# Moving the first step of a float64-to-float32 conversion from VectorE to ScalarE in a fused attention and gated-MLP kernel, with a new order of all instructions

## The chip, the core and the metric

The kernel runs on one core of a Trainium2 chip. Five engines work side by side, each in the order of its own instruction queue: TensorE (PE in the profile; its weight loads are PEld), VectorE (DVE), ScalarE (ACT), GpSimd (POOL) and SyncE (SP), which issues nearly all DMA transfers. The metric is the device time of one execution in microseconds, and the median over several executions is compared.

## The reference

A recurrence with decay runs over 768 positions for 4 x 8 heads of width 48, and its output goes through a gated MLP with 384 inputs and 1536 hidden units, for all 3072 tokens:

```python
for t in range(S):
    state = alpha[:, :, t, :, None] * state + np.einsum('bhd,bhe->bhde', k[:, :, t], v[:, :, t])
    y[:, :, t] = np.einsum('bhd,bhde->bhe', q[:, :, t], state)
...
g = x @ w_gate
silu = g * (1.0 / (1.0 + np.exp(-g)))
val = x @ w_val
return (silu * val @ w_out).astype(np.float32)
```

q, k, v and alpha are float32. The three weight matrices reach the kernel as float64, that is as pairs of 32-bit words, because they were drawn as float32 and then scaled with a float64 number.

## The kernel before, in words

**Attention.** The sequence is cut into 16 units of 192 positions (4 per batch element), each of three chunks of 64. The words of a unit u in the order table are: loads `La`, `Lk`, `Lq`, `V`; for the first four units a widening copy `pa`, `pk`, `pq` (L382), a transposition on TensorE `Ta`, `Tk`, `Tq` (L394) and evacuations `ea`, `ek`, `cq` (L798); for the later units a transposition on VectorE (`tr`, `tk`, `tq`, L374). `G` is the backward scan of the decays (L439) and `f` the forward scan after it (L445, L448), with a small reset `z`. `mk` and `q` multiply k and q with the scanned decays. `S` are the scores, `ma` their masking (L567), `K` and `kc` turn k and copy it out of PSUM, `B` and `Bw` form the carries between chunks, `ad` and `de` advance the state, `Y` are the outputs. `yh` and `yl` split an output into a high part rounded to float32r and the rest, and `R`, `x` (on chip) or `xr` (by DMA) lay it out as the MLP's input tile xT. Two units make one block of 384 tokens.

**MLP.** 96 steps s go over 8 blocks and 12 slices f of 128 hidden units. Blocks 0 and 1 alternate: steps 0 to 6 are block 0 with f 0 to 6, steps 7 to 13 block 1 with the same f, then f 7 to 11 of both. `g` and `v` are the products with the gate and the value weights, nine matmuls each, since both operands are split into high and low parts and three of the four combinations are used; `sl` is the silu on ScalarE (L710), `h` the product on VectorE (L714), `hh` and `hl` its high and low part (L718, L723), `o` the nine matmuls with `w_out` (L734). Each of `g` and `v` has one PSUM bank, so `v` of a step waits for `h` of the step before.

**Weights.** 36 pieces of 128 x 384 weights are loaded once, in 20 groups; groups 0, 1, 2 and 19 hold one piece (384 words per partition), the others two (768). Group 0 is the gate slice of f 0, 1 the value slice of f 0, 2 the gate slice of f 1, 3 the value slice of f 1 and the output slice of f 0, and so on. `wl` loads the raw words; the raw words of a group lie in the place of the next group's result, so that one cannot be written before the other is converted. Three conversion steps `w..v0`, `w..v1`, `w..v2` build a float32 word in a tile t (three buffers, shared with the range checks), all on VectorE (L148, L151, L154). `w..a` rounds it to float32r (L321), `w..p` subtracts for the low part (L325). Later each piece is loaded a second time (`wr`) and its range checked by ScalarE (`wc`, two activations that add up what lies outside, L296 and L297). If the sums are not as they should be, a slower general path runs behind the main one. `Lc` and `ck` do the same for alpha.

**What sets the order.** The table `ORDER` lists every word with its engine (t TensorE, v VectorE, s ScalarE, g GpSimd, y SyncE) and, behind @, the PSUM banks. The words are issued in the table's order, each engine runs its own in that order, and semaphores hold an instruction until its operands are there. Nothing is reordered.

Of the kernel before, what the change touches and what calls it, by code (L numbers as in the profile page):

```python
# [44 lines left out]
v:G0 s:w1a y:Lk1 s:pa1 y:La2 s:pq0 t:Ta1@01 v:w1p y:Lk2 t:Tq0@23 v:f0 g:z0 s:pk0 y:V0 t:Tk0@45 s:pq1 v:q0 g:pk1 g:w0p
v:mk0 t:Tk1@23 s:ea1 y:Lq2 s:ek1 t:Tq1@45 v:G1 y:La3 t:S0@01 y:wl2 s:qc0 y:wl3 t:K0.0@2 s:pa2 t:K0.2@3 v:f1 g:z1
s:kc0.0 t:K0.1@6 y:Lk3 s:vc0 y:wl4 s:kc0.1 y:wl5 v:ma0.2 g:mk1 s:kc0.2 t:Ta2@26 s:pa3 y:wl6 t:Bw0@1 v:w2v0 s:cq1
v:w2v1 y:wl7 v:w2v2 g:q1 t:K1.2@3 v:ma0.0 s:ad0.1 t:K1.1@4 t:K1.0@5 v:ma0.1 s:kc1.2 y:wl8 s:kc1.1 v:w3v0 s:qc1 t:S1@34
v:w3v1 s:ad0.2 v:w3v2 y:wl9 s:ea2 v:de1 s:ad0.0 t:Ta3@02 v:G2 s:kc1.0 t:Y0@16 y:wl10 s:pk2 s:w3a v:f2 g:z2 t:Bw1@5
s:yh0.0 y:V2 s:yh0.1 s:vc1 v:yl0.0 g:w3p s:ad1.0 v:ma1.0 s:ad1.1 v:ma1.2 v:yl0.1 t:Tk2@14 g:pq2 v:ma1.1 t:R0.2@6 g:w2a  # L50
v:mk2 s:ad1.2 s:x0.2 v:w2p t:Y1@35 v:w4v0 v:w5v0 t:Tq2@14 v:w5v1 y:V3 s:yh1.0 t:R0.1@6 s:yh1.1 v:w6v0 s:cq2 v:w4v1
s:pk3 t:K2.1@1 v:w4v2 t:R0.0@4 s:x0.1 s:kc2.1 t:K2.0@6 v:yl1.1 g:q2 s:w4a t:K2.2@1 v:x0.0 v:yl1.0 t:Tk3@45 s:kc2.0
y:Lq3 v:de2 s:kc2.2 y:wl11 t:R1.1@3 s:ea3 t:R1.2@6 v:w6v1 y:wl12 t:R1.0@1 v:w6v2 s:x1.2 t:S2@02 s:vc2 y:wl13 v:G3
# [88 lines left out]
def single(nc, raw, t):  # L142

    lo, hi = raw[:, :, 0], raw[:, :, 1]
    return [
        lambda: nc.vector.tensor_scalar(  # L148
# [958 lines left out]
```

## Time and profile before

| What | Value |
|---|---|
| Median of 3 executions | 576.37 us (576.31 to 577.98) |
| The profiled execution's own time | 574.98 us |
| Its span, first to last instruction | 573.2 us |
| Busy: PE, DVE, ACT, POOL | 546.3, 385.0, 248.4, 147.0 us |
| Mean granted TensorE clock | 0.989 |
| HBM read, written | 62.52 MB, 5.90 MB |

A row of a group of instructions reads: line, engine, operation, output and input tiles, shape, count, then total busy time and the mean of one in ns, then the idle time before them and what released most of it. A row of the timeline reads: start, duration, engine, line, operation, count, and in brackets the idle time before it with its releaser. A row of the table by stages gives the stretch and its length, the busy time and count of PE, PEld, DVE, ACT and POOL, the granted clock, the DMA share and GB/s. The chain gives start, length and what it was.

### The profile page before, as it was taken

To read this page: it belongs to the slowest core of one execution; us is meant where nothing else is said; L and a number is where in the kernel's file an instruction comes from. 1 tells how busy PE (TensorE), PEld (TensorE's weight loads), DVE (VectorE), ACT (ScalarE), POOL (GpSimd) and SP (SyncE) were. 2 spreads that over 40 slices of the span, in tenths; PEclk is the share of its full clock that TensorE was granted. 3 is DMA by queue.
4 is the path that set the end of the run, shared out by engine and by line. 5 is a ranking of instruction groups with operands and counts; after the bars stand their busy time and mean duration, and the time that the engine had idled before them with its cause. 6 is when DMAs were issued, how large, how long until landed. Compare 5 with 4: busy or idle time off the path is not lost.

```text
span 573.2 us, 13708 instructions
## 1 busy us (share of the span) xinstructions
PE 546.3 (95%) x5510; PEld 527.2 (92%) x5510; DVE 385.0 (67%) x596; ACT 248.4 (43%) x573; POOL 147.0 (26%) x169
## 2 busy tenths in 40 slices
...
GB/s 238 270 307 250 247 125 145 43 115 81 86 147 164 136 117 107 124 91 145 170 169 191 172 181 132 179 110 102 207 125 123 128 151 63 94 76 59 0 1 47
...
## 3 DMA queue, kind: packets, MB, share of 16 engines
...
HBM read 62.52 MB, written 5.90 MB: 119 GB/s over the span
## 4 chain that ended last, share of the span: by engine, by line
PE 88%; DVE 4%; ACT 2%; SPq 2%; issue 1%; DMA 1%; DVEq 0%; ACTq 0%
PE v L702 26%; PE ops L734 26%; PE g L702 25%; PE A L557 3%; PE y L629 2%; PE s L533 2%; PE pt L394 1%; SPq L686 1%; PE y L612 1%; PE y L613 1%; DVE t L154 1%; DVE t L151 1%; DMA raw<-in_moe_w_val_dram 1%; DVE w L325 1%; PE s L557 1%
## 5 line engine op out<-in xcount | busy, mean ns | idle before, releaser
L702 PE MATMUL v<-xT,w 128*128 128x384 f32 x864 | 167.6, 338 | 3.3 <-DVE h L714 3.3
L702 PE MATMUL g<-xT,w 128*128 128x384 f32 x864 | 166.9, 337 | 0.0
L734 PE MATMUL ops<-w,hh 128*128 128x384 f32 x576 | 158.8, 337 | 0.0
L702 PEld LDWEIGHTS v<-xT,w 128*128 128x128 f32 x864 | 150.5, 188 | 5.2 <-DVE h L714 4.4
L702 PEld LDWEIGHTS g<-xT,w 128*128 128x128 f32 x864 | 150.9, 188 | 0.6
L723 POOL TENSOR_TENSOR hl<-h,hh 128x384 fp32r<-128x384 f32 x67 | 70.5, 1052 | 250.3 <-ACT hh L718 236.0
L714 DVE TENSOR_TENSOR h<-h,v 128x384 f32<-128x384 f32 x96 | 53.0, 552 | 119.0 <-PE v L702 106.6
L718 ACT CAST hh<-h 128x384 fp32r<-128x384 f32 x96 | 49.0, 512 | 150.9 <-DVE h L714 77.5
L734 PEld LDWEIGHTS ops<-w,hh 128*128 128x128 f32 x576 | 105.3, 188 | 0.9 <-ACT K L497 0.2
L734 PE MATMUL ops<-w,hl 128*128 128x384 f32 x288 | 96.7, 336 | 0.0
L710 ACT ACTIVATE h<-g 128x384 f32<-128x384 f32 x96 | 47.0, 490 | 114.1 <-PE g L702 102.9
L508 DVE STREAM_TRANSPOSE K<-Gs 32x384 f32<-32x384 f32 x96 | 54.7, 570 | 5.4 <-PE A L557 3.8
L734 PEld LDWEIGHTS ops<-w,hl 128*128 128x128 f32 x288 | 54.1, 188 | 0.0
L567 DVE TENSOR_TENSOR X<-s,mask 64x384 f32<-64x384 f32 (+1 forms) x48 | 26.0, 550 | 5.8 <-DMA wc<-in_moe_w_out_dram 3.4
L439 DVE TENSOR_TENSOR_SCAN Gs<-AT,inj 128x772 f32<-128x772 f32 x16 | 29.0, 1814 | 1.1 <-ACT AT L798 0.8
L448 DVE TENSOR_TENSOR_SCAN AT<-AT,back 128x771 f32<-128x771 f32 x16 | 29.2, 1824 | 0.7
L723 DVE TENSOR_TENSOR hl<-h,hh 128x384 fp32r<-128x384 f32 x29 | 16.1, 557 | 16.3 <-ACT hh L718 16.2
L394 PE MATMUL pt<-ident,wide 128*128 128x128 f32 x72 | 14.2, 352 | 13.1 <-ACT wide L382 8.2
L394 PEld LDWEIGHTS pt<-ident,wide 128*128 128x128 f32 x72 | 10.7, 181 | 15.4 <-POOL sel L348 5.1
L452 POOL MEMSET AT<- 128x3 f32 x16 | 1.7, 106 | 89.1 <-DVE AT L448 89.1
L297 ACT ACTIVATE wc<-wc,wbias 128x384 f32<-128x384 f32 x36 | 23.3, 647 | 1.2
L325 POOL TENSOR_TENSOR w<-t,w 128x768 fp32r<-128x768 f32 (+1 forms) x11 | 19.1, 1744 | 15.3 <-ACT w L321 15.0
...
## 6 DMA issues: line engine op xcount, KB each, us to landing
...
raw<-in_moe_w_gate_dram SPq DMA_DIRECT2D x12, 384.0 KB, 8.0
raw<-in_moe_w_val_dram SPq DMA_DIRECT2D x12, 384.0 KB, 7.8
...
raw<-in_moe_w_out_dram SPq DMA_DIRECT2D x12, 384.0 KB, 7.8
wc<-in_moe_w_gate_dram SPq DMA_DIRECT2D x12, 384.0 KB, 5.0
wc<-in_moe_w_val_dram SPq DMA_DIRECT2D x12, 384.0 KB, 3.7
wc<-in_moe_w_out_dram SPq DMA_DIRECT2D x12, 384.0 KB, 3.9
```

Of the source, the lines that this page charges most:

```text
L325: eng.tensor_tensor(out=lo, in0=src, in1=hi.bitcast(F32), op=ALU.subtract)
L394: nc.tensor.transpose(pt[:, j - js.start, :], Wd.rearrange("p j e c -> p (j e c)")[:, j * P : (j + 1) * P], ident)
L439: nc.vector.tensor_tensor_scan(*(x.rearrange("p g t -> p (g t)")[:, ::-1] for x in (Gs, AT, inj)), 0.0, op0=ALU.mult, op1=ALU.add)
L448: nc.vector.tensor_tensor_scan(Af, Af, back[:, 1 : n + 1], back[:, 0:1], op0=ALU.mult, op1=ALU.add)
L508: nc.vector.transpose(out=bass.AP(k0.tensor, k0.offset, [k0.ap[0], (G * 2 * D, NU), (2 * D, G), (1, 32)]), in_=Kg[j * BO + x : j * BO + x ...
L567: nc.vector.tensor_tensor(out=X[r, z, f * GF : (f + 1) * GF, :].rearrange("r g (c t) -> r g c t", c=NU), in0=sps[f][r].rearrange("r g (c t ...
L702: nc.tensor.matmul(pt, wsp[kind, f][a][:, kt * P : (kt + 1) * P], xT[blk][:, b_, kt, :], start=(n == 0), stop=(n == 3 * KT - 1),)
L710: nc.scalar.activation(h, acc.pop(("g", blk, f)), AF.Silu)
L714: nc.vector.tensor_tensor(out=h, in0=h, in1=acc.pop(("v", blk, f)), op=ALU.mult)
L718: nc.scalar.copy(out=hh, in_=acc["h", blk, f])
L723: eng.tensor_tensor(out=hl, in0=acc.pop(("h", blk, f)), in1=hh.bitcast(F32), op=ALU.subtract)
L734: nc.tensor.matmul(ops[blk][i], h[b_][:, i * P : (i + 1) * P], wsp["o", f][a], start=(first and n == 0), stop=(last and n == 2),)
```

## The change

Three things are changed.

First, the conversion may begin on ScalarE. Before, VectorE's first step shifts the upper word left by 3 and sets bits, the second masks with the upper word, and the third brings in the top three bits of the lower word by a shift. Now, where the table names s for `w..v0`, ScalarE reads the lower word as a number, multiplies it with 7.49 / 2^32 and writes the result as an integer, 0 to 7, which stands for those three bits; VectorE then shifts the upper word, joins it, and masks. Where the table names v, VectorE does three steps as before, the last two exchanged.

Second, since the bits that were set before are now taken from the word itself, the range check must also exclude large weights. It takes |x|, then the distance from the middle of the permitted range, then what this exceeds half the range by: three activations instead of two.

Third, the order was searched anew, with an eighth PSUM bank (`ops2`) open for the early transpositions, turned pieces of k and outputs; the dummy matmuls, of which the table held none, are removed with the bank that they kept.

```diff
+W_LEAST, W_MOST = 4.0e-5, 1.9999
+W_MID, W_DEV = (W_MOST + W_LEAST) / 2, (W_MOST - W_LEAST) / 2
+LOW3 = 7.49 / 2.0 ** 32
...
 ORDER = """
-y:La0 y:wl0 y:wl1 y:Lq1 y:La1 y:Lq0 y:Lk0 s:pa0 y:V1 t:Ta0@01 v:w0v0 v:w0v1 s:ea0 v:w0v2 v:w1v0 v:w1v1 s:w0a v:w1v2
...
+y:La0 y:wl0 y:Lk1 y:La1 y:Lq0 y:V1 s:pa0 t:Ta0@01 s:w0v0 v:w0v1 s:ea0 v:w0v2 y:Lk0 s:w0a v:G0 s:pa1 y:Lq1 s:pq0 y:La2
...
     lo, hi = raw[:, :, 0], raw[:, :, 1]
...
+    def first(eng):
+        by.append(eng)
+        if eng is nc.scalar:
+            eng.activation(t, lo, AF.Copy, scale=LOW3)
+        else:
+            eng.tensor_scalar(
+                out=t, in0=hi, scalar1=3, scalar2=0xC0000001, op0=ALU.logical_shift_left, op1=ALU.bitwise_or
+            )
+
+    def second(eng):
+        if by[0] is nc.scalar:
+            eng.scalar_tensor_tensor(
+                out=t, in0=hi, scalar=3, in1=t, op0=ALU.logical_shift_left, op1=ALU.bitwise_or
+            )
+        else:
+            eng.scalar_tensor_tensor(
+                out=t, in0=lo, scalar=29, in1=t, op0=ALU.logical_shift_right, op1=ALU.bitwise_or
+            )
+
+    def third(eng):
+
+        eng.scalar_tensor_tensor(
             out=t, in0=hi, scalar=0x3FFFFFFF, in1=t, op0=ALU.bitwise_or, op1=ALU.bitwise_and
...
         nc.scalar.activation(dev, dev, AF.Abs, accum_out=wviol[:, 1, i : i + 1])
-        nc.scalar.activation(dev, dev, AF.Relu, bias=wbias, scale=-1.0, accum_out=wviol[:, 0, i : i + 1])
+        nc.scalar.activation(dev, dev, AF.Abs, bias=wbias[:, 0:1])
+        nc.scalar.activation(dev, dev, AF.Relu, bias=wbias[:, 1:2], accum_out=wviol[:, 0, i : i + 1])
...
-    BANKS = ("A0", "A1", "A2", "ops0", "ops1", "vps", "gps")
+    BANKS = ("A0", "A1", "A2", "ops0", "ops1", "vps", "gps", "ops2")
```

What the table now orders stands below at three places. A row names the line, the operation, the output and input tiles with their numbers, and the output's shape.

The first is the start of VectorE's queue, from the first conversion to the second backward scan (tiles: t and w are the conversion's and its result, Gs the scan's, AT the decays, pt a transposed bank, X a masked q, back the forward scan's factors). Before, the rows from the first conversion on:

```order
L148 TENSOR_SCALAR t0_155<-raw0_132 128x384
L151 SCALAR_TENSOR_TENSOR t0_155<-raw0_132,t0_155 128x384
L154 SCALAR_TENSOR_TENSOR t0_155<-raw0_132,t0_155 128x384
L148 TENSOR_SCALAR t1_161<-raw1_134 128x384
L151 SCALAR_TENSOR_TENSOR t1_161<-raw1_134,t1_161 128x384
L154 SCALAR_TENSOR_TENSOR t1_161<-raw1_134,t1_161 128x384
L439 SCALAR_TENSOR_TENSOR Gs0_167<-AT_86,inj_74 128x772
L325 TENSOR_TENSOR w1_169<-t1_161,w1_169 128x384
L445 RECIPROCAL back_89<-Gs0_167 128x4
L448 SCALAR_TENSOR_TENSOR AT_86<-AT_86,back_89 128x771
```

and now:

```order
L165 SCALAR_TENSOR_TENSOR t0_152<-raw0_132,t0_152 128x384
L175 SCALAR_TENSOR_TENSOR t0_152<-raw0_132,t0_152 128x384
L462 SCALAR_TENSOR_TENSOR Gs0_161<-AT_86,inj_74 128x772
L468 RECIPROCAL back_89<-Gs0_161 128x4
L471 SCALAR_TENSOR_TENSOR AT_86<-AT_86,back_89 128x771
L475 MEMSET AT_86 128x3
```

Group 0 has two steps there instead of three, and group 1 is converted after the second forward scan.

The second is ScalarE's queue around the evacuation of unit 2's decays (`ea2`, the rows that write AT). Before (kps and K: turned k and its copy; A2, s and SE: the carries and the state; wide: a widening copy):

```order
L473 COPY X1_104<-X1_104 48x384
L588 COPY SE_109<-s0_0_243 48x96 x2
L588 COPY SE_109<-A2_0_323 48x96 x2
L798 COPY AT_86<-pt2_0_0_311 128x4x32x3
L798 COPY AT_86<-pt2_0_1_315 128x4x32x3
```

and now:

```order
L496 COPY X1_104<-X1_104 48x384
L157 ACTIVATE t2_387<-raw2_221 128x384
L157 ACTIVATE t3_390<-raw3_223 128x768
L519 COPY K0_105<-kps1_0_315 64x4x48
L520 COPY K0_105<-kps1_0_315 64x4x48
L604 COPY V0_77<-A2_0_331 48x8x48
L604 COPY V0_77<-A2_0_331 48x8x48
L343 CAST w1_430<-t1_383 128x384
L343 CAST w2_435<-t2_387 128x384
L810 COPY AT_86<-pt2_0_0_285 128x4x32x3
L810 COPY AT_86<-pt2_0_1_289 128x4x32x3
```

Two first steps and two casts of the conversion, one turned piece and the advance of the state now stand between `qc1` and `ea2`; the copies into SE came before `ea2` and come after it now.

The third is TensorE's queue around the first gate product g0. Before (y: outputs of unit 2; kps3: a turned piece of unit 3's k):

```order
L629 MATMUL y1_2_855<-X0_103,U_101 48x64
L629 MATMUL y1_2_855<-X0_103,V0_77 48x64
L702 MATMUL g0_0_903<-xT0_587,w0_164 128x384 x9
L492 MATMUL kps3_1_920<-ident_91,Gs3_765 64x112 x4
L702 MATMUL v0_0_925<-xT0_587,w1_169 128x384 x9
L702 MATMUL g0_1_945<-xT0_587,w2_591 128x384 x9
```

and now:

```order
L515 MATMUL kps3_1_840<-ident_91,Gs3_750 64x112 x4
L725 MATMUL g0_0_845<-xT0_576,w0_159 128x384 x9
L725 MATMUL v0_0_867<-xT0_576,w1_430 128x384 x9
L635 MATMUL y0_2_890<-X0_103,V0_77 64x64
L636 MATMUL y0_2_890<-X0_103,V0_77 48x64
L635 MATMUL y1_2_891<-X0_103,V0_77 64x64
```

The outputs of unit 2 stood ahead of g0 and stand behind v0 now; one turned piece of unit 3's k has come ahead of it.

More of the change, by code (lines that the diff above doesn't have):

```diff
@@ L43 @@
 ORDER = """
-y:La0 y:wl0 y:wl1 y:Lq1 y:La1 y:Lq0 y:Lk0 s:pa0 y:V1 t:Ta0@01 v:w0v0 v:w0v1 s:ea0 v:w0v2 v:w1v0 v:w1v1 s:w0a v:w1v2
[L45 to L53, printed above, removed]
@@ new lines @@
+t:Ta1@01 y:V0 v:f0 t:Tq0@23 s:pk1 s:pk0 t:Tk1@45 v:z0 v:q0 t:Tk0@67 v:w0p s:qc0 y:wl1 v:mk0 g:pq1 s:ea1 y:wl2 y:wl3
+s:ek1 t:Tq1@23 v:G1 t:K0.0@0 y:wl4 s:pa2 t:S0@14 s:kc0.0 y:Lk3 v:mk1 t:K0.1@5 s:vc0 t:Ta2@67 y:La3 v:ma0.2 t:K0.2@0
+s:cq1 y:wl5 v:f1 t:K1.2@4 s:kc0.1 t:K1.0@2 y:wl6 t:K1.1@3 s:kc0.2 v:q1 t:Bw0@0 y:wl7 v:w1v0 s:qc1 v:w1v1 s:w2v0 v:w1v2
+s:w3v0 v:w2v1 y:wl8 s:kc1.0 v:w2v2 s:ad0.1 v:ma0.0 g:z1 t:S1@25 v:w3v1 s:w1a y:wl9 s:ad0.0 s:w2a v:ma1.2 g:pa3 s:ea2
+v:ma0.1 v:w1p s:ad0.2 t:Ta3@56 v:G2 y:Lk2 s:w4v0 t:Y0@01 y:Lq2 s:kc1.2 v:de1 s:kc1.1 y:wl10 v:f2 s:yh0.0 t:Bw1@3
@@ new lines @@
+s:yh0.1 y:V2 v:yl0.0 g:vc1 v:yl0.1 s:ad1.0 s:ad1.1 g:z2 v:ma1.0 t:R0.2@0 v:ma1.1 t:R0.1@1 v:w2p s:x0.2 t:Y1@47 s:ad1.2
+v:w4v1 v:w4v2 s:w5v0 s:x0.1 v:w5v1 t:R0.0@0 v:w5v2 s:yh1.0 s:pk2 y:wl11 v:yl1.0 s:pq2 v:w3v2 t:Tk2@12 s:w5a t:Tq2@34
+v:mk2 g:w4a s:w3a y:Lq3 y:wl12 s:x0.0 v:q2 g:w3p t:K2.2@1 s:yh1.1 t:K2.1@0 y:V3 s:kc2.2 t:K2.0@2 v:yl1.1 t:S2@34
+s:kc2.1 v:de2 s:ea3 t:R1.1@0 v:ma2.2 g:pk3 t:R1.0@1 s:kc2.0 v:x1.1 t:R1.2@4 v:G3 s:x1.0 t:Tk3@02 s:x1.2 t:Bw2@1 s:pq3
+y:wl13 s:vc2 v:mk3 y:wl14 s:w6v0 v:f3 t:Tq3@02 s:qc2 y:wl15 s:ad2.1 t:K3.1@4 t:g0 y:wl16 s:cq3 v:w6v1 y:wl17 s:kc3.1
```

206 lines of the change are left out of this document (94 added, 112 removed).

## The prediction

> **What bounds the kernel now.** I read the page's totals first, then the same totals by stage, then what TensorE (PE) waits for, then VectorE (DVE) in order of time.
>
> ```profile
> PE 546.3 (95%) x5510; PEld 527.2 (92%) x5510; DVE 385.0 (67%) x596; ACT 248.4 (43%) x573; POOL 147.0 (26%) x169
> core 0: us, PE busy (x) PEld busy (x) DVE busy (x) ACT busy (x) POOL busy (x), PEclk, DMA share, GB/s
> 0.00:26.00 26.00, 15.41 (x258) 13.16 (x258) 18.21 (x30) 17.63 (x36) 12.84 (x32) 1.00 0.83 242
> 26.00:34.00 8.00, 6.29 (x126) 5.46 (x128) 7.72 (x11) 5.67 (x14) 0.31 (x2) 0.60 1.08 368
> ...
> 44.00:48.00 4.00, 2.86 (x11) 2.86 (x12) 3.90 (x8) 2.98 (x7) 0.52 (x1) 0.58 0.43 67
> 48.00:56.20 8.20, 6.38 (x224) 5.49 (x223) 7.30 (x12) 6.19 (x15) 2.02 (x2) 1.00 1.01 348
> 56.20:97.30 41.10, 37.83 (x364) 35.56 (x361) 36.49 (x47) 19.32 (x40) 10.88 (x11) 1.00 0.70 177
> 97.30:300.00 202.70, 202.70 (x2203) 196.81 (x2204) 182.61 (x278) 58.19 (x127) 74.05 (x75) 1.00 0.49 121
> 300.00:550.00 250.00, 250.00 (x2088) 245.74 (x2087) 116.49 (x198) 128.26 (x312) 40.38 (x42) 1.00 0.44 121
> 550.00:573.20 23.20, 16.44 (x95) 16.12 (x93) 3.19 (x6) 4.46 (x9) 1.02 (x1) 0.94 0.08 29
> ```
>
> From 97.3 to 550 us PE is busy in every microsecond at the full granted clock. No TensorE work is added or removed, so that stretch cannot shrink; it can only start earlier, or gain holes. The idle of PE lies ahead of it (10.6 us before 26, about 9.6 us from 26 to 97.3) and in the last 23 us (6.8). The change therefore is worth what it does to the moment at which the dense stretch begins, which I mark by the product v7 (the first value product of block 1).
>
> ```profile
> 91.87 3.25 DMA L<-in_alpha_dram
> ...
> 95.25 0.06 DVE AT L374
> ...
> 96.67 0.56 DVE h L714
> ...
> 97.27 1.86 PE v L702 x9
> ```
>
> These are pieces of the chain of work that ended last. v7 starts at 97.27 because DVE's multiplication h6 ran at 96.67, behind a transposition (`tr4`) that waited for a load of alpha that SyncE had issued at 91.87. So in this stage DVE, and through it the DMA queue, releases PE. DVE's own order of time tells where it stood:
>
> ```profile
> 8.43 1.78 DVE L439 TENSOR_TENSOR_SCAN Gs<-AT,inj 128x772 f32<-128x772 f32 x1
> 15.54 1.77 DVE L439 TENSOR_TENSOR_SCAN Gs<-AT,inj 128x772 f32<-128x772 f32 x1 [0.85 <-ACT AT L798]
> 23.67 0.59 DVE L148 TENSOR_SCALAR t<-raw 128x384 uint32<-128x384 uint32 x1 [3.84 <-DMA raw<-in_moe_w_gate_dram]
> 29.72 1.77 DVE L439 TENSOR_TENSOR_SCAN Gs<-AT,inj 128x772 f32<-128x772 f32 x1
> 41.70 2.46 DVE L154 SCALAR_TENSOR_TENSOR t<-raw,t 128x768 uint32<-128x768 uint32 x1
> 48.11 1.76 DVE L439 TENSOR_TENSOR_SCAN Gs<-AT,inj 128x772 f32<-128x772 f32 x1
> 60.13 0.56 DVE L714 TENSOR_TENSOR h<-h,v 128x384 f32<-128x384 f32 x1 [0.76 <-PE v L702]
> ```
>
> The four backward scans G0 to G3 start at 8.43, 15.54, 29.72 and 48.11, and h0 at 60.13. Those, and v7, are my milestones.
>
> **What each edit costs.** The rows by shape:
>
> ```profile
> L148 DVE TENSOR_SCALAR t<-raw 128x768 uint32<-128x768 uint32 x16 | 10.2, 654 | 0.8 <-POOL w L325 0.8
> L151 DVE SCALAR_TENSOR_TENSOR t<-raw,t 128x768 uint32<-128x768 uint32 x16 | 16.6, 1042 | 0.3
> L148 DVE TENSOR_SCALAR t<-raw 128x384 uint32<-128x384 uint32 x4 | 1.7, 417 | 5.2 <-DMA raw<-in_moe_w_gate_dram 5.1
> L321 ACT CAST w<-t 128x768 fp32r<-128x768 f32 x14 | 11.6, 832 | 11.9 <-DVE t L154 11.9
> L321 ACT CAST w<-t 128x384 fp32r<-128x384 f32 x2 | 1.0, 504 | 0.8 <-DVE t L154 0.8
> L827 POOL TENSOR_TENSOR Gs<-trk,Gs 128x768 f32<-128x768 f32 x9 | 15.4, 1714 | 8.3 <-DVE trk L374 4.8 <-DVE Gs L439 3.5
> L827 DVE TENSOR_TENSOR Gs<-trk,Gs 128x768 f32<-128x768 f32 x4 | 3.8, 953 | 0.1
> L296 ACT ACTIVATE wc<-wc 128x384 f32<-128x384 f32 x36 | 19.8, 550 | 0.0
> ```
>
> *The first step on ScalarE (ACT).* The new order gives it 16 of the 20 groups (14 wide, 2 narrow). DVE is freed of 14 x 0.654 + 2 x 0.417 = 10.0 us over the program. No row shows an ACTIVATE from uint32 to uint32; the nearest is ACT's own cast, 0.83 and 0.50 us, so 14 x 0.83 + 2 x 0.50 = 12.6 us more on ACT. Bounds: nothing (it hides on an engine that is 43% busy) and the whole 12.6 us, if each copy stood ahead of something that PE wants. I take it as hidden save at one place, below.
>
> The Trainium skill, "ScalarE: Activation LUTs", section "Rules for kernel authors", says that multiplications and the like belong on VectorE rather than ScalarE. The rows agree that ACT is slower, 0.83 against 0.65 us. By that rule the move would lose 12.6 - 10.0 = 2.6 us if ACT were the engine waited for (the second rival); by the rows, DVE is at 36.5 of 41.1 us between 56 and 97 and ACT at 19.3.
>
> *The third activation of each range check.* 36 x 0.55 = 20 us more on ACT, nearly all between 300 and 550 us, where ACT is busy 128 of 250 us and PE never waits for it: cost 0; without that cover at most one check's 0.55 us ahead of each silu, of which PE could lose a few.
>
> *The order.* Half of the words move, and ahead of h6 the freed time is partly spent: DVE now takes `mk1`, `q1` and `q2` from GpSimd (POOL), at 0.95 instead of 1.71 us each, and conversions stand earlier. Adding each DVE instruction up to and with h6 at its uncontended duration (scan 1.80, forward scan with reciprocal 2.0, `mk` and `q` 0.95, conversion steps 0.50 and 0.97, narrow 0.37 and 0.58, low part 0.95, other elementwise 0.47 to 0.50, transposition 1.6) gives 77.3 us before and 74.8 now: a saving of only 2.5 us. Where it falls:
>
> - *To G1.* V1's six loads now stand ahead of `Lk0`; by SP's pace of 0.65 us per load k0 is issued at about 8.2, and its widening shares a buffer with alpha's. `mk0` can run at 14.8 and G1 at 15.75 instead of 15.54: 0.2 us lost, though G0 starts at 8.1, since w1's three steps no longer stand before it.
> - *To G2.* Before, DVE stood idle for 3.84 us until group 2's words landed. Now `mk1`, `ma0.2`, `f1`, `q1` (4.4 us) fill that. From G1 on DVE has 11.8 us of work, so 27.6; but G2 needs `ea2`, and on ACT that stands behind `w3v0`, which needs group 3's words. Their last load is issued at about 16.4. With the 8.0 us that a weight load took to land
>
> ```profile
> raw<-in_moe_w_gate_dram SPq DMA_DIRECT2D x12, 384.0 KB, 8.0
> ```
>
>   they come at 24.4; then `w3v0` 0.83, `kc1.0` 2 x 0.31, `ad0.1` 2 x 0.47, two narrow casts 1.0 and `ea2` 2 x 0.5 by the rows
>
> ```profile
> L581 ACT COPY V<-A 48x384 f32<-48x384 f32 x8 | 3.8, 473 | 2.7 <-PE A L557 2.6
> L496 ACT COPY K<-kps 64x192 f32<-64x192 f32 x12 | 3.7, 311 | 0.3
> ```
>
>   and G2 starts at 28.8 to 29.2. Lead 0.7 us.
> - *To G3.* The work between is 16.4 us, before 16.0 (18.4 less 0.9 of wait and 1.5 of the stretched step at 41.70). A wait of about 2 us for the carry `Bw1` takes the place of that: `ad0.2` and `kc1.1` are late on ACT, so Y0 starts at 30.2, and I give it the 3 us (29.16 to 32.13) and `Bw1` the 2.8 us (32.13 to 34.92) that they took before at a granted clock of 0.6:
>
> ```profile
> 29.16 0.28 PE y L612
> ...
> 32.13 2.09 PE A L557 x48
> 34.22 0.70 PE s L557 x24
> ```
>
>   G3 at about 47.5: lead still 0.7.
> - *g0 and h0.* The outputs Y2 now come after v0. x1 is ready near 48.9; Bw2 2.4, Tq3 0.9, one transposition 0.4: g0 near 52.6, h0 near 55.8.
> - *To v7.* PE has after v0: Y2 2.2, S3 1.0, two turned pieces 0.9, Bw3 2.4, Y3 2.2 and 18 products of 1.57
>
> ```profile
> 100.71 1.59 PE g L702 x9
> ```
>
>   = 28.3, together 37.0: v7 at 92.9. DVE has 31.9 us from h0 to h6, 1.4 of waiting for v1, and stretches. At 41.70 a step took 2.46 instead of 0.96 us while POOL ran a multiplication, and two more were stretched by 0.8 and 1.6 us:
>
> ```profile
> 41.66 1.69 POOL L467 TENSOR_TENSOR X<-trq,AT 112x768 f32<-112x768 f32 x1 [4.99 <-ACT trq L798]
> 61.47 1.76 DVE L154 SCALAR_TENSOR_TENSOR t<-raw,t 128x768 uint32<-128x768 uint32 x1
> 88.16 2.21 DVE L148 TENSOR_SCALAR t<-raw 128x768 uint32<-128x768 uint32 x1
> ```
>
>   Together 3.9 us before; I count 3 to 4 here. h6 near 92.5, v7 near 93.5 to 94. The late alpha load is gone: SP is through with block 1's repacking near 85, and `tr4` stands behind h7. Lead at v7: 97.3 - 93.8 = 3.5 us.
> - *After v7* the same products remain. The PE work up to each later v, less the DVE work up to the h that frees its bank, leaves at least 2.0 us for v8 to v59, before 1.1, and before did not stall. So the lead is kept, and the last 23 us end in the same way (o93, o94, o95, three output tiles).
>
> **Sum.** 573.2 - 3.5 = 569.7 us of span, 571.5 for the profiled execution (574.98 before). That execution lay 1.4 us below the median of 576.37, so the forecast is 576.37 - 3.5 = 572.9 us.
>
> **Rivals.**
>
> *A larger lead (chance 0.18).* If group 3's words land by 22 and the clock isn't cut around Y0 and Bw1, the 2 us wait before G3 and the 1.5 us on ACT vanish, and with few stretches v7 starts near 90.3: 569.4 us. For it: the clock row 26 to 34 shows 0.60 only after PE had idled. Against it: PE idles there in the new order too, from S1 to Ta3.
>
> *ScalarE's order eats the lead (0.18).* ACT now holds thirteen copies ahead of h6 that wait for a DMA or for a conversion buffer, and in-order evacuations stand behind them (`kc`, `ad`, `yh`, each released to PE). If `w3v0`, `w5v0` and `w3a` each hold ACT 1 us longer than I count, the lead of 3.5 is 0.5: 575.9, no change. Against it: ACT was idle for half of that stage.
>
> *Slower: GpSimd against DVE's conversions (0.18).* Ahead of v7 POOL now casts w4 and w6, subtracts w3, w6 and w7 and makes hl0, hl1 and hl3 to hl6, and the conversions that DVE keeps are the kind that was stretched at 41.70. Each hit costs 0.8 to 1.6 us, 1.3 in the mean. I count three; from seven on (4 x 1.3 = 5.2 us more, the lead and 1.7 us) it is slower, and at eight, 6.5 us more, 579.4 us. For it: all three places above lay beside a POOL instruction, and there are eleven such now. Against: of most groups one step in three has left DVE.
>
> The Trainium skill, "SBUF — State Buffer", section "SBUF: two separate sides", states the mechanism: GpSimd and VectorE have one port pair in common, an exclusive lock, which a VectorE instruction with two SBUF inputs also needs. The trace agrees at 41.70 and 61.47. By that rule the scans and the products `mk1`, `q1` and `q2` could be hit as well, where I count conversions alone; each would count as one more hit.
>
> That the first step isn't moved can be excluded: the order of ACT shows 16 of them.
>
> **How the numbers follow.** The forecast (lead 1.8 to 5.2, so 571.2 to 574.6) has 0.46, the rivals 0.18 each. 0.3% is 1.7 us, about what a measurement can tell from no change. Faster: 0.46 + 0.18 = 0.64; same: 0.18; slower: 0.18. Eight in ten: from 568.0, a little beyond the larger lead, to 578.0, which leaves out the worst of the port rival.
>
> **What would show it.** G1 near 15.8, G2 near 29, G3 near 47.5, g0 near 52.6 ahead of Y2, v7 at 93 to 95 with no DMA wait ahead of h6; PE at 100% after that; ACT near 281 us busy, DVE near 375. Wrong if PE has holes after 100 us, if ACT's copies take over 1 us, if the conversions' mean on DVE rises above 1.1 us, or if G2 comes after 31 us.

## The result, and the profile after

| | before | after |
|---|---|---|
| Median, 7 executions each | 576.79 us (576.01 to 578.50) | 573.60 us (572.48 to 574.62) |
| Ratio, 95% interval | | 0.9935 (0.9916 to 0.9954) |
| Profiled execution, its span | 574.98, 573.2 us | 572.89, 570.8 us |

The change is 0.65% faster, 3.75 us by the ratio. The forecast was 3.5 us less, 572.9 us.

First the page's totals of the changed kernel, then its table by stages (stretch and length, busy time and count of PE, PEld, DVE, ACT and POOL, granted clock, DMA share, GB/s):

```profile
PE 545.7 (96%) x5510; PEld 527.4 (92%) x5510; DVE 391.7 (69%) x601; ACT 280.5 (49%) x621; POOL 134.0 (23%) x152
```

```profile
26.00:34.00 8.00, 5.25 (x144) 4.65 (x146) 7.81 (x11) 6.88 (x19) 0.86 (x2) 0.79 1.08 364
...
56.20:97.30 41.10, 38.75 (x400) 36.34 (x390) 37.34 (x43) 24.28 (x44) 15.19 (x13) 1.00 0.65 167
97.30:300.00 202.70, 201.43 (x2149) 194.48 (x2148) 186.01 (x281) 56.01 (x117) 64.65 (x64) 1.00 0.47 114
300.00:550.00 250.00, 250.00 (x2135) 246.21 (x2134) 119.45 (x204) 153.98 (x360) 38.56 (x36) 1.00 0.47 127
550.00:570.80 20.80, 14.19 (x82) 13.87 (x80) 2.78 (x5) 3.89 (x8) 1.01 (x1) 0.89 0.10 32
```

PE is busy all the time from 300 to 550 us as before, but from 97.3 to 300 it now lacks 1.27 us, where it lacked nothing. The milestones, from VectorE's and TensorE's order of time:

```profile
16.19 2.00 DVE L462 TENSOR_TENSOR_SCAN Gs<-AT,inj 128x772 f32<-128x772 f32 x1
29.82 1.75 DVE L462 TENSOR_TENSOR_SCAN Gs<-AT,inj 128x772 f32<-128x772 f32 x1
47.34 1.76 DVE L462 TENSOR_TENSOR_SCAN Gs<-AT,inj 128x772 f32<-128x772 f32 x1
55.17 0.55 DVE L737 TENSOR_TENSOR h<-h,v 128x384 f32<-128x384 f32 x1 [1.08 <-ACT SE L611]
92.78 0.55 DVE L737 TENSOR_TENSOR h<-h,v 128x384 f32<-128x384 f32 x1
```

```profile
51.67 1.83 PE L725 MATMUL g<-xT,w 128*128 128x384 f32 x9
...
93.38 1.86 PE L725 MATMUL v<-xT,w 128*128 128x384 f32 x9 [0.45 <-DVE h L737]
...
266.99 1.84 PE L725 MATMUL v<-xT,w 128*128 128x384 f32 x9 [1.25 <-DVE h L737]
```

These are G1 to G3, h0 and h6, then g0, v7 and one v far behind. v7 comes 3.89 us earlier than before (97.27). Of that, 1.25 us is lost at 266.99, 0.40 is spread over single starts behind v7 and not followed further, and the last part (from PE's end, 564.20, to the end of the span) is 0.16 us shorter: 3.89 - 1.25 - 0.40 + 0.16 = 2.40 us, the difference of the two spans. The medians differ by more, since each profile is one execution; in the profiles of the runs below that leave the stretch ahead of v7 nearly as it is, v7 lies between 92.30 and 94.93.

The hole at 267 has its cause in DVE's and POOL's order of time:

```profile
264.44 1.91 DVE L746 TENSOR_TENSOR hl<-h,hh 128x384 fp32r<-128x384 f32 x1
266.39 0.55 DVE L737 TENSOR_TENSOR h<-h,v 128x384 f32<-128x384 f32 x1
```

```profile
264.24 1.70 POOL L490 TENSOR_TENSOR X<-trq,AT 112x768 f32<-112x768 f32 x1 [7.23 <-DMA out_dram<-ot]
```

hl37 takes 1.91 us on DVE, where the median of its kind is 0.56, because POOL's product q10 runs from 264.24 to 265.94; h38 stands behind it, and v39 waits for h38.

The rows by shape that answer to those the costs were taken from:

```profile
L157 ACT ACTIVATE t<-raw 128x768 uint32<-128x768 uint32 x14 | 12.7, 916 | 1.4 <-DVE w L347 1.3
L157 ACT ACTIVATE t<-raw 128x384 uint32<-128x384 uint32 x2 | 1.1, 552 | 0.0
L165 DVE SCALAR_TENSOR_TENSOR t<-raw,t 128x768 uint32<-128x768 uint32 x14 | 16.5, 1180 | 0.5 <-ACT t L157 0.4
L318 ACT ACTIVATE wc<-wc,wbias 128x384 f32<-128x384 f32 x36 | 23.3, 648 | 1.2
```

### The profile page after: what moved, and what is told of

It reads as the page before. It is cut to its first block, busy times and chain, and to the rows that moved or that the text cites. A ratio compares the mean times of both kernels' runs of the same rounds, so it can differ in the third digit from the quotient of the medians.

```text
span 570.8 us, 13758 instructions
## 1 busy us (share of the span) xinstructions
PE 545.7 (96%) x5510; PEld 527.4 (92%) x5510; DVE 391.7 (69%) x601; ACT 280.5 (49%) x621; POOL 134.0 (23%) x152
## 4 chain that ended last, share of the span: by engine, by line
PE 76%; DMA 10%; DVE 7%; SPq 3%; issue 2%; ACT 1%; DVEq 0%; ACTq 0%
PE ops L757 24%; PE v L725 23%; PE g L725 22%; DMA raw<-in_moe_w_out_dram 3%; DMA raw<-in_moe_w_gate_dram 2%; PE y L652 2%; PE A L580 2%; PE s L556 2%; DMA raw<-in_moe_w_val_dram 1%; DMA L<-in_k_dram 1%; DMA Le<-in_q_dram 1%; DVE K L531 1%; SPq L436 1%; PE y L635 1%; DVE t L165 1%
## 5 line engine op out<-in xcount | busy, mean ns | idle before, releaser
L737 DVE TENSOR_TENSOR h<-h,v 128x384 f32<-128x384 f32 x96 | 52.9, 551 | 120.1 <-PE v L725 92.5
L746 POOL TENSOR_TENSOR hl<-h,hh 128x384 fp32r<-128x384 f32 x57 | 65.5, 1150 | 264.7 <-ACT hh L741 263.5
L746 DVE TENSOR_TENSOR hl<-h,hh 128x384 fp32r<-128x384 f32 x39 | 22.9, 589 | 14.8 <-ACT hh L741 14.6
L471 DVE TENSOR_TENSOR_SCAN AT<-AT,back 128x771 f32<-128x771 f32 x16 | 30.9, 1933 | 0.6
L417 PEld LDWEIGHTS pt<-ident,wide 128*128 128x128 f32 x72 | 12.1, 197 | 13.4 <-ACT wide L405 5.1
L319 ACT ACTIVATE wc<-wc,wbias 128x384 f32<-128x384 f32 x36 | 23.4, 650 | 1.2
L318 ACT ACTIVATE wc<-wc,wbias 128x384 f32<-128x384 f32 x36 | 23.3, 648 | 1.2
L839 POOL TENSOR_TENSOR Gs<-trk,Gs 128x768 f32<-128x768 f32 x10 | 17.9, 1785 | 25.3 <-DVE Gs L462 13.8
## 6 DMA issues: line engine op xcount, KB each, us to landing
raw<-in_moe_w_gate_dram SPq DMA_DIRECT2D x12, 384.0 KB, 7.5
raw<-in_moe_w_val_dram SPq DMA_DIRECT2D x12, 384.0 KB, 7.9
raw<-in_moe_w_out_dram SPq DMA_DIRECT2D x12, 384.0 KB, 7.5
wc<-in_moe_w_gate_dram SPq DMA_DIRECT2D x12, 384.0 KB, 4.8
wc<-in_moe_w_val_dram SPq DMA_DIRECT2D x12, 384.0 KB, 3.5
wc<-in_moe_w_out_dram SPq DMA_DIRECT2D x12, 384.0 KB, 3.4
```

Source lines behind the costliest of these rows:

```text
L319: nc.scalar.activation(dev, dev, AF.Relu, bias=wbias[:, 1:2], accum_out=wviol[:, 0, i : i + 1])
L417: nc.tensor.transpose(pt[:, j - js.start, :], Wd.rearrange("p j e c -> p (j e c)")[:, j * P : (j + 1) * P], ident)
L471: nc.vector.tensor_tensor_scan(Af, Af, back[:, 1 : n + 1], back[:, 0:1], op0=ALU.mult, op1=ALU.add)
L737: nc.vector.tensor_tensor(out=h, in0=h, in1=acc.pop(("v", blk, f)), op=ALU.mult)
L746: eng.tensor_tensor(out=hl, in0=acc.pop(("h", blk, f)), in1=hh.bitcast(F32), op=ALU.subtract)
```

## The experiments

The theory: the gain is the lead at v7; it needs both the first step on ScalarE and the new order; the third activation of the range checks costs nothing; what limits the lead is GpSimd and VectorE in each other's way. The rivals: the order alone, or the offload alone, gives it; or the lead is bounded by loads.

### The parts alone

e1, the new order with every first step on VectorE (all 16 words `s:w..v0`):

```diff
-... t:Ta0@01 s:w0v0 v:w0v1 ...
+... t:Ta0@01 v:w0v0 v:w0v1 ...
```

> The changed kernel with the first step of all 16 groups given back to VectorE; the new order, the eight banks and the three-activation range check stay. Ahead of h6 these are 11 wide and 2 narrow steps, 11 x 0.65 + 2 x 0.42 = 8.0 us more on DVE. Theory (the gain is the offload's): DVE is what v7 waits for, so v7 comes 5 to 8 us later than 93.4 (some of the 8.0 fills DVE's waits ahead of G2 and G3) and the time is 578 to 581 us, slower than the kernel before by 0.3 to 0.8%. Rival (the gain is the new order's, the offload hides in waits): v7 stays ahead of 96 and the time is at most 575 us.

e2, the order of before with the same 16 first steps on ScalarE (`v:w0v0` to `s:w0v0` and so on, in the old table):

> The order of the kernel before, with the first step of the same 16 groups on ScalarE: the offload alone, seven banks. Theory (offload and order need each other): DVE is freed of about 8 us ahead of h6, but h6 stands behind tr4, whose load of alpha SyncE issued at 91.87 in the kernel before, and G2 waits for weights; v7 comes 0 to 2 us ahead of 97.27, so 575 to 577 us. Rival (the offload alone brings it): v7 at 94 or earlier, 573.5 us or less. Second rival (ScalarE's order eats the lead): evacuations behind copies that wait for weights, v7 after 98, 578 us or more.

e3, the order of before as it was, in the changed code:

> The order of the kernel before with every first step on VectorE, in the code of the change: against the kernel before only the third activation of each range check (36 more on ScalarE) and the turn of the second and third conversion step differ. Theory (these cost nothing): 576.8 us, ratio 1.000 within 0.002, ACT about 20 to 23 us busier between 300 and 550 us, PE without holes there. Rival (a third activation ahead of a silu costs PE): 0.5 us for each of a few silus, 578 to 580 us, with holes of PE between 300 and 550.

e5, as e3, with the range check of before, so that large weights aren't looked for:

```diff
-        nc.scalar.activation(dev, dev, AF.Abs, bias=wbias[:, 0:1])
-        nc.scalar.activation(dev, dev, AF.Relu, bias=wbias[:, 1:2], accum_out=wviol[:, 0, i : i + 1])
+        nc.scalar.activation(dev, dev, AF.Relu, bias=wbias[:, 0:1], scale=-1.0, accum_out=wviol[:, 0, i : i + 1])
```

> The order of the kernel before, every first step on VectorE, in the code of the change, but with the range check of two activations as before (the check of large weights is left out). With the third activation this order took 580.4 us and PE had two new holes behind late silus, 1.06 us at 301 and 0.27 us at 423. Theory (the third activation ahead of a silu makes them): both holes go, 1.3 to 2.7 us less, 577.5 to 579 us, ratio 1.000 to 1.003. Rival (the turn of the conversion's steps costs the 3 us): 580 us again, ratio 1.005.

| order | first step on | activations | median us | ratio to before (95%) | DVE busy |
|---|---|---|---|---|---|
| old (e5) | DVE | 2 | 576.91 | 1.0004 (0.9980 to 1.0028) | 384.0 |
| old (e3) | DVE | 3 | 580.42 | 1.0055 (1.0020 to 1.0090) | 385.4 |
| old (e2) | ACT | 3 | 579.51 | 1.0041 (1.0020 to 1.0061) | 375.0 |
| new (e1) | DVE | 3 | 578.31 | 0.9998 (0.9976 to 1.0020) | 398.3 |
| new (the change) | ACT | 3 | 573.60 | 0.9935 (0.9916 to 0.9954) | 391.7 |

**The offload needs the order.** Under the old order the offload brings nothing that can be told apart (1.0041 against 1.0055), under the new one 0.6%. The order is worth something by itself: in the same code, with every first step on VectorE, it takes the ratio from 1.0055 (e3) to 0.9998 (e1), which makes good what the third activation costs under the old one. Together the two bring 1.2%, one by one 0.1 and 0.6%; the 0.5% that is left over for their working together is about as large as the uncertainty of the four ratios. Two more programs weren't run: the new order with two activations, and an order searched for first steps on VectorE.

In e1's profile v7 comes at 100.21, 6.8 us behind the changed kernel's; the 8.0 us of conversion steps that the offload takes from DVE ahead of h6 return almost whole there. But this execution was the slowest of e1's twelve (580.41 us, median 578.31), and the ratios differ by 0.63%, which is 3.6 us. The time was no slower than before, 0.9998, where 0.3 to 0.8% slower was expected; the theory's direction held, its size was too large (578.31 us lies at the low end of its 578 to 581). In e2 the steps on ScalarE wait, and others with them. From ACT's and DVE's order of time in e2:

```profile
25.03 0.54 ACT L156 ACTIVATE t<-raw 128x384 uint32<-128x384 uint32 x1 [1.68 <-DMA raw<-in_moe_w_gate_dram]
```

```profile
57.02 0.96 DVE L164 SCALAR_TENSOR_TENSOR t<-raw,t 128x768 uint32<-128x768 uint32 x1 [2.58 <-ACT t L156]
```

ACT stands 1.68 us behind a load of weights, DVE 2.58 us behind ACT's step, h0 comes at 65.83 and v7 at 101.16. That is the rival in which ScalarE's order eats the lead, in an order that was not made for it; e2's 579.51 us is above the 575 to 577 that the theory expected of it. In the changed kernel ACT never stands behind a load in these steps (the row L157 above: 1.4 us of idle time in all, 1.3 of it behind DVE).

**The third activation is not free.** e3 is 0.55% slower than before, e5 is not, though their two intervals touch. e3's 580.42 us is the rival, just beyond its 578 to 580 us; e5's 576.91 is the theory, a little below its 577.5 to 579. TensorE's order of time in e3 has two holes that before did not have:

```profile
301.49 1.83 PE L724 MATMUL g<-xT,w 128*128 128x384 f32 x9 [1.06 <-ACT h L732]
...
423.53 1.86 PE L724 MATMUL g<-xT,w 128*128 128x384 f32 x9 [0.27 <-ACT h L732]
```

and ACT ahead of the first of them:

```profile
299.62 0.67 ACT L317 ACTIVATE wc<-wc,wbias 128x384 f32<-128x384 f32 x1
300.33 0.65 ACT L318 ACTIVATE wc<-wc,wbias 128x384 f32<-128x384 f32 x1
...
300.96 0.47 ACT L732 ACTIVATE h<-g 128x384 f32<-128x384 f32 x1
```

Three range checks stand close ahead of it; each is 0.65 us longer, so the silu behind them is late and g waits for its bank. With two activations (e5) neither hole is there; e2, with three, has both again (1.06 us at 304.23, 0.27 at 426.37). The holes explain 1.3 of the 2.9 us that lie between the two ratios; the rest isn't located. In the changed kernel there is no wait for a silu behind v7: there the new order hides the third activation, and the prediction's 0 holds for that order alone.

### The hole at 267

e4, hl37 on GpSimd in the same place, so that it runs ahead of q10 on the same engine:

```diff
-s:sl38 v:ad9.2 t:g39 v:hl37 s:ot35.2 v:h38 ...
+s:sl38 v:ad9.2 t:g39 g:hl37 s:ot35.2 v:h38 ...
```

> The changed kernel with one word moved: the low part hl37 on GpSimd, in the same place, so that it stands ahead of the product q10 on GpSimd and no longer beside it on VectorE. In the changed kernel hl37 took 1.91 us on DVE beside q10 (POOL 264.24 to 265.94) instead of 0.55, h38 came 1.4 us late and PE lost 1.25 us at 267. Theory (the port hit makes the hole): the hole at 267 us goes, 1.2 us less than the changed kernel, 572.3 us, ratio 0.9915. Rival (PE lacks the time there anyway, or it is lost again later): the wait for h38 stays or reappears, 573.5 us.

Measured: 571.84 us, ratio 0.9906 (0.9876 to 0.9937), and no wait of PE at 267. From DVE's and POOL's order of time in e4:

```profile
264.45 0.56 DVE L737 TENSOR_TENSOR h<-h,v 128x384 f32<-128x384 f32 x1
```

```profile
263.87 1.70 POOL L490 TENSOR_TENSOR X<-trq,AT 112x768 f32<-112x768 f32 x1 [0.30 <-DMA out_dram<-ot]
```

h38 runs wholly beside the same q10 and isn't stretched; one of its operands, v, lies in PSUM, while hl37 had both in SBUF. The Trainium skill, "SBUF — State Buffer", section "SBUF: two separate sides", says that a VectorE instruction takes the port pair it has in common with GpSimd where it has two SBUF inputs, and that the loser waits for the whole of the other's instruction; both rows agree, and hl37's end at 266.35 is q10's end plus 0.41 us.

This execution of e4 also began quicker (below), v7 stood at 92.30, and another hole opened. From its DVE and PE:

```profile
96.91 1.65 DVE L397 STREAM_TRANSPOSE AT<-L 128x768 f32<-128x768 f32 x1 [2.11 <-DMA L<-in_alpha_dram]
...
102.56 0.53 DVE L737 TENSOR_TENSOR h<-h,v 128x384 f32<-128x384 f32 x1
```

```profile
103.14 1.86 PE L725 MATMUL v<-xT,w 128*128 128x384 f32 x9 [1.15 <-DVE h L737]
```

h8 stands behind the transposition tr4, the scan G4 and the scan f4, and tr4 waits 2.11 us for alpha. In the changed kernel that load is no earlier, only hidden better: there v7 stood later and tr4 waited 0.80 us. SyncE's and DVE's order of time there:

```profile
82.05 7.08 SPq L709 DMA_DIRECT2D xT<-X  x10
```

```profile
96.71 1.68 DVE L397 STREAM_TRANSPOSE AT<-L 128x768 f32<-128x768 f32 x1 [0.80 <-DMA L<-in_alpha_dram]
```

SP is through with block 1's repacking at 89.1, issues the load for unit 5 first and then the one that tr4 needs.

e8, with hl37 moved and that put right: the load of alpha for unit 4 ahead of that for unit 5, and h8 ahead of f4:

```diff
-... v:w11v2 y:La5 v:h5 ... s:sl6 y:La4 t:o4 ... t:o6 v:f4 t:g9 s:ot6.0 s:ot6.1 v:h8 g:hl7 ...
+... v:w11v2 v:h5 ... s:sl6 y:La4 y:La5 t:o4 ... t:o6 t:g9 s:ot6.0 s:ot6.1 v:h8 v:f4 g:hl7 ...
```

> The changed kernel with hl37 on GpSimd as in the run before, and two more moves: the load of alpha for unit 4 ahead of that for unit 5, and h8 ahead of the forward scan f4 on VectorE. In the run with hl37 alone h8 stood behind tr4, G4 and f4, tr4 waited 2.11 us for the alpha load, and PE lost 1.15 us at 103 ahead of v9. Theory (the next bound after v7 is this alpha load): h8 comes 2 us or more ahead of need, no hole at 103 even where the start is early, 1.1 us less than with hl37 alone in such executions and none in others: 571.0 us, ratio 0.9895. Rival (the gain is given back at the next h): PE has a hole between 97 and 120 again, 571.8 us, ratio 0.9906.

Measured: 571.95 us, ratio 0.9911 (0.9884 to 0.9938); tr4 waits 0.20 us, h8 starts at 100.51, and PE has no hole from 97 to 560. The time is that of e4 within the intervals, and the number is the rival's (571.8), though the hole that the rival expected isn't there. So it is shown that these moves close the hole behind tr4, and not what they are worth in the time. The hole isn't bound to a quick start: e7 (below) started slowly, tr4 waited 2.60 us there, and PE lost 1.41 us.

How the holes cap the lead is seen from where PE ends. In the changed kernel, e11, e6 and e7 v7 comes at 93.38, 93.75, 94.93 and 94.04, and PE ends at 564.20, 564.00, 564.24 and 564.81: the two with the earlier v7 have the hole at 267, the other two have not, and 1.5 us of difference in v7 leave 0.8 at the end. In e6 q10 starts at the same time as in the changed kernel, 264.29, but hl37 comes later, at 265.60, and takes 0.81 us: the hit is only as large as what is left of q10. With hl37 moved PE ends at 562.69 (e4) and 562.79 (e8). In e8 v7 comes at 93.93, no earlier than in the changed kernel, so its earlier end isn't owed to the start.

### GpSimd against VectorE ahead of v7

e7, one low part on VectorE instead of GpSimd:

```diff
-t:Y3@01 v:h2 g:w7p s:w9a v:tk4 ...
+t:Y3@01 v:h2 v:w7p s:w9a v:tk4 ...
```

> The changed kernel with one low part, w7p, on VectorE instead of GpSimd. In the changed kernel GpSimd ran it from 66.94 for 2.61 us, and beside it a conversion step of VectorE took 2.59 instead of 0.95 us. Theory (the port is what stretches both): that step takes under 1.1 us, DVE pays 0.95 us for w7p, so h3 comes 0.5 to 0.7 us earlier or nearly so, and the time is 573.0 us, ratio 0.9925; at most 1 us is to be had. Rival (DVE's work, not the port, decides there): the step is as short, but h3 to h6 come no earlier or later, 573.6 to 574.5 us.

Measured: 572.80 us, ratio 0.9924 (0.9897 to 0.9950). The changed kernel's POOL and DVE around 67 us:

```profile
66.94 2.61 POOL L347 TENSOR_TENSOR w<-t,w 128x768 fp32r<-128x768 f32 x1 [4.60 <-ACT w L343]
69.52 1.73 POOL L746 TENSOR_TENSOR hl<-h,hh 128x384 fp32r<-128x384 f32 x1
```

```profile
66.90 0.96 DVE L175 SCALAR_TENSOR_TENSOR t<-raw,t 128x768 uint32<-128x768 uint32 x1
67.78 2.59 DVE L165 SCALAR_TENSOR_TENSOR t<-raw,t 128x768 uint32<-128x768 uint32 x1
70.40 1.66 DVE L175 SCALAR_TENSOR_TENSOR t<-raw,t 128x768 uint32<-128x768 uint32 x1
71.98 0.54 DVE L737 TENSOR_TENSOR h<-h,v 128x384 f32<-128x384 f32 x1
```

and e7's DVE:

```profile
69.90 0.95 DVE L165 SCALAR_TENSOR_TENSOR t<-raw,t 128x768 uint32<-128x768 uint32 x1
70.88 0.96 DVE L175 SCALAR_TENSOR_TENSOR t<-raw,t 128x768 uint32<-128x768 uint32 x1
71.76 0.55 DVE L737 TENSOR_TENSOR h<-h,v 128x384 f32<-128x384 f32 x1
```

The engines take turns, an instruction each: w7p is held up by the step before, the next step (2.59 us) by w7p, hl1 by that step, the last step (1.66) by hl1. With w7p gone both steps take their 0.95 us. From h1 to h3 DVE needs 14.70 us instead of 15.34, though it has w7p's own 0.95 to do: the 0.6 us that were expected. v7 came no earlier in that one execution (94.04), since v1 was 1.3 us later than in the changed kernel, and PE lost 1.41 us at 105, with h8 behind tr4 again. So the step is shown, and what it is worth in the time isn't told apart from the start.

### The start

e6, the load of k0 ahead of the six of V1 (`y:V1` moved behind `y:Lk0`):

> The changed kernel with the load of k0 ahead of the six loads of V1 instead of behind them. In the changed kernel mk0 waited 1.75 us for Tk0 and G1 started at 16.19. Theory (SyncE's order costs the start): k0 is issued near 4.3 instead of 8.2, mk0's wait falls below 0.5 us, G1 comes at 14.5 to 15.2 and v7 about 1 us earlier: 572.5 us, ratio 0.992. Rival (the start waits for q1, for the clock and for the weights, not for k0): G2 and v7 as in the changed kernel, 573.6 us, ratio 0.9935.

Measured: 573.61 us, ratio 0.9945 (0.9924 to 0.9966): the rival. k0 is issued at 4.24 instead of 8.20, and mk0 waits the same 1.75 us. What it waits for is the pace of the transpositions, first in the changed kernel, then in e4, whose instructions are the same up to there:

```profile
12.86 2.82 PE L417 MATMUL pt<-ident,wide 128*128 128x128 f32 x12 [0.81 <-ACT wide L405]
```

```profile
12.99 1.53 PE L417 MATMUL pt<-ident,wide 128*128 128x128 f32 x12 [0.81 <-ACT wide L405]
```

Twelve transpositions take 2.82 us or 1.53, with the granted clock at 1.00 in both. In the slow case G1 comes at 16.1 to 16.4 and G2 at 29.6 to 30.6 (the changed kernel, e1, e6, e7, e11; e1's VectorE has more to do there, the others end at 30.0), in the quick one at 15.0 to 15.2 and 27.0 to 28.2 (e4, e8, e10).

What makes a start quick or slow isn't shown. The only program that was profiled twice, the changed kernel (again as e11), started slowly both times, and the three quick starts are the three programs with hl37 on GpSimd, although that word is issued some 250 us later. (Of the two runs with zeros below, too, the one with hl37 on GpSimd, e12, has the quick second dozen.) With one profile each, chance can't be told from a cause in the program. Nor is a quick start kept: it leads by 1.4 to 3.0 us at G2 and by 0.8 to 1.8 at G3 (46.29, 46.58 and 45.95 in e4, e8 and e10, 47.34 to 47.70 in the slow ones without e1). In between, in the quick starts, GpSimd's widening copy pa3 waits for the alpha of unit 3, which lands no earlier than in a slow start (the copy runs at 26.67 in e10, at 26.90 in the changed kernel), and the transposition Ta3 waits for this copy on TensorE.

e9 keeps TensorE busy from the start, with 13 matmuls of zeros that nothing uses:

```diff
+            nc.tensor.matmul(early_ps, busy[:, 0:P], busy.unsqueeze(1).to_broadcast([P, 2, 2 * P]), start=True, stop=True)
...
-... s:pa0 t:Ta0@01 s:w0v0 ...
+... s:pa0 t:8* t:Ta0@01 t:5* s:w0v0 ...
```

> The changed kernel with 13 matmuls of zeros of 128 x 512 (bf16) that nothing uses, 8 ahead of TensorE's first transpositions (Ta0) and 5 behind them, into the eighth bank, so that TensorE is busy from about 1.3 us on. In the changed kernel 12 transpositions took 2.82 us at 9.23 and again at 12.86; in two later runs the second dozen took 1.53. Theory (TensorE runs at half speed until it has been busy for some microseconds, whatever the granted clock says): both dozens take 1.5 to 1.6 us, mk0's wait of 1.75 us falls below 0.8, G1 comes at 14 to 15, v7 0.5 to 1.5 us earlier: 572.5 us, ratio 0.9925. Rival (the transpositions wait for their operands, or the lost time comes back at G2, whose weights are late anyway): the dozens may be short, but G2 stays above 29 and v7 above 93, 573.6 us.

Measured: 576.01 us, ratio 0.9980 (0.9957 to 1.0002), worse than either side expected. From e9's PE, and its table by stages:

```profile
5.09 0.84 PE L418 MATMUL pt<-ident,wide 128*128 128x128 f32 x6 [0.62 <-POOL mask L244]
...
12.28 2.82 PE L418 MATMUL pt<-ident,wide 128*128 128x128 f32 x12 [0.81 <-ACT wide L406]
...
61.31 0.57 PE L516 MATMUL kps<-ident,Gs 112*64 112x112 f32 x4 [3.11 <-issue]
```

```profile
12.00:18.00 6.00, 4.78 (x22) 4.25 (x22) 4.68 (x7) 3.84 (x8) 0.66 (x1) 0.50 0.75 188
```

The first six transpositions do take 0.84 us (1.51 without the zeros): with the zeros ahead of them TensorE is quick. But then the granted clock falls to 0.50, the second dozen is as slow as ever, and G1 comes at 15.61. Up to h0 nothing is gained and nothing lost (55.41, in e11 55.38). Then, from 58 us on, a hole of 3.11 us opens for which the profile names no releaser; v1 starts at 64.38 (61.07) and v7 at 97.42 (93.75). So nearly all of the lost time is this hole, and the early cut of the clock cost nothing that is still seen at h0.

e11 is the changed kernel again, e10 all four moves of e7 and e8 together, e12 these and the zeros.

> The changed kernel as it is, beside the others of this batch: 573.6 us, ratio 0.9935 within 0.002, one hole of 1.2 us ahead of a v near 267. If its start is the quick one (the second dozen of transpositions in 1.5 us), v7 comes near 92.3 and a hole near 103 takes that back.

> The changed kernel with all the moves that helped or did no harm: hl37 on GpSimd, the alpha load of unit 4 ahead of that of unit 5, h8 ahead of f4, w7p on VectorE. Theory (the hole at 267, the waits behind tr4 and the stretched steps are separate losses): no hole of PE from 97 to 560, h3 0.6 us earlier than without w7p's move, 571.0 us, ratio 0.990. Rival (they overlap): as with hl37 alone, 571.8 us, ratio 0.991 to 0.992.

> All the moves of the run before and the 13 matmuls of zeros. Theory (a quicker start is kept once the alpha load no longer holds h8): 0.5 to 1 us less than without the matmuls, 570.2 us, ratio 0.9885. Rival (the start's gain is lost to the clock that is cut between 26 and 34 us or to the weights): 571 us.

| | median us | ratio to before (95%) | v7 | PE's waits for h, 97 to 560 |
|---|---|---|---|---|
| e11 | 573.52 | 0.9948 (0.9928 to 0.9968) | 93.75 | 1.14 at 267 |
| e10 | 570.37 | 0.9888 (0.9864 to 0.9911) | 92.34 | none |
| e12 | 574.95 | 0.9961 (0.9940 to 0.9983) | 96.43 | none |

e10 beats the changed kernel as its theory expected, by a little more; the two intervals don't meet. e12 lies 4 us or more above both of its expectations. From e10's table by stages:

```profile
97.30:300.00 202.70, 202.70 (x2230) 196.38 (x2228) 184.72 (x281) 56.36 (x117) 65.59 (x64) 1.00 0.47 118
300.00:550.00 250.00, 250.00 (x2072) 246.47 (x2067) 117.64 (x203) 153.48 (x359) 38.56 (x36) 1.00 0.45 124
```

PE is dense again behind v7. PE ends at 561.15 and in e11 at 564.00: of these 2.85 us 1.41 are the earlier v7 and 1.14 the hole. e10's profile is one with a quick start, so the 1.41 us are not the moves' alone. In e12 both dozens of transpositions were quick and G2 came at 26.94 (26.96 in e10), yet G3 at 47.81 (45.95). The clock doesn't tell the two apart: it was 0.72 from 26 to 30 and 0.50 from 30 to 34 us in e12, 0.50 and 0.69 in e10. The load of unit 3's alpha does, first in e10, then in e12:

```profile
26.67 0.89 POOL L405 COPY wide<-L 128x576 f32<-128x576 f32 x1 [6.15 <-DMA L<-in_alpha_dram]
```

```profile
27.85 1.31 POOL L406 COPY wide<-L 128x576 f32<-128x576 f32 x1 [7.99 <-DMA L<-in_alpha_dram]
```

Ta3, which waits for this copy, starts at 27.62 in e10 and at 29.22 in e12: 1.6 of the 1.9 us by which G3 is later. Further on a hole of 2.59 us without a releaser opened ahead of kps again.

The eighth bank wasn't tried alone. By the table the transposition Ta2 holds two banks, the eighth among them, from before Bw0 until `ea2`; with seven, some other word of that stretch would have to wait for a bank. No run shows what that would cost, and what the bank gives is part of what the order gives.

## Why the prediction was right, point by point

- **What bounds, and the lead at v7: right.** Forecast v7 at 93.5 to 94, h6 at 92.5, g0 at 52.6, h0 at 55.8, G3 at 47.5; measured 93.38, 92.78, 51.67, 55.17, 47.34. The sum of 3.5 us stands against 3.75 by the ratio and 3.2 by the medians. That v7 fits so closely is in part luck: G2 was 0.6 to 1.0 us later than forecast and G3 was not, h0 came 0.6 us earlier, and the stretches ahead of h6 then took some 2 us more than was counted. Of the lead only 1.2 us is less work: from 4.2 us up to and with h6 DVE is busy for 79.9 us before and for 78.7 now; the other 2.7 us are waits of DVE that the new order fills.
- **G1 and G2: the time was near by luck, the reason wrong.** G2 was forecast for 28.8 to 29.2, because `ea2` would stand on ACT behind `w3v0`, and that behind group 3's words. It came at 29.82, 0.1 us behind the kernel before instead of 0.7 ahead. No word was late: in the quick start of e4 ACT ran the first steps of groups 2 and 3 at 22.14 already; in the changed kernel they ran at 24.59, behind `qc1`, which had waited for DVE's q1. DVE itself ran from 20.46 to G2 without a wait. What was late was TensorE: both dozens of its transpositions ran at about half the pace, and DVE waited 1.75 us for Tk0 and 1.20 us for the scores S0. The prediction took no account of that. The step that failed is "To G2" with its load of 8.0 us.
- **DVE near 375 us: wrong, 391.7.** Under the old order the offload frees what was said (e3 to e2: 10.4 us, forecast 10.0), under the new one, stretches included, 6.6 (e1 to the changed kernel: 398.3 to 391.7). What failed is that 375 holds only what the offload frees, and not what the new order gives back to DVE: 12.9 us over the program (e3 to e1: 385.4 to 398.3), among it ten more low parts (39 instead of 29). Ahead of h6 the prediction had counted word by word, and that held: 2.5 us less, measured 2.2 (79.9 to 78.7 us, less stretches of 4.6 and 5.6).
- **ACT: right in sum, 280.5 for 281, by luck.** Each price was too low: 0.92 and 0.55 us for the first step, forecast 0.83 and 0.50; the activation with a pointer as bias 0.65, forecast 0.55. By the rows that is 13.8 + 23.3 = 37.1 us, but ACT's total rose by 32.1, in part because the order took some 2.8 us of casts and copies off it; the rest wasn't followed. The work was hidden, as forecast: PE waits for no silu behind v7, and ahead of it once, 0.39 us at 76.44.
- **The third activation at 0: right here, wrong as a rule.** Under the old order e3 lies 0.5% above e5.
- **"No holes after v7": wrong.** The slack of at least 2.0 us was PE's work less DVE's work, at undisturbed durations. At 267 DVE also waited 1.85 us for S9 and its carries, and hl37 was stretched by 1.35 us. The prediction had this mechanism as a rival ahead of v7 and didn't carry it behind v7, where it took a third of the lead. That was one of the prediction's own signs of being wrong; a second was met by a hair, with the conversions' mean on DVE above 1.1 us (the row L165 has 1.18; all wide steps with two inputs have 1.11).
- **"The late alpha load is gone": wrong.** SP ended the repacking at 89.1 and not near 85, and the load for unit 5 stood in front. Being behind h7 it cost nothing in the changed kernel's two profiles and in e6's, 1.15 us in e4's and 1.41 us in e7's.
- **The rivals.** GpSimd in DVE's way was the one nearest to the truth: ahead of h6 seven steps were stretched, by some 5.6 us together, where three hits and 3 to 4 us were counted and seven were to make it slower. Two things kept it from being slower. A hit was smaller than the 1.3 us that were taken, 0.8 in the mean. And the kernel before had four hits ahead of h6, not three: at 68.64 two steps took 2.52 us together beside a `hl`, some 0.7 too long. So the stretches grew by 1.0 us only, from 4.6 to 5.6. ScalarE's order eating the lead was seen in e2 alone. The larger lead came in two of the three quick starts, 1.1 us of it (v7 at 92.30 in e4 and 92.34 in e10, but 93.93 in e8), and not by early weights.
